# Whole products with diagonal blocks used in place, an earlier load, and two max terms on GpSimd, in a linear-attention and SwiGLU kernel

## The chip, the cores and the metric

The kernel runs on one core of a Trainium2 chip. The metric is the device time of one execution in microseconds (us), the slowest core's; here there is only one. A time is about 2 us longer than the span of the profile of the same execution. Engines are named as the profile names them: PE (TensorE matmuls), PEld (its weight loads), DVE (VectorE), ACT (ScalarE), POOL (GpSimd), SP.

## The reference

Linear attention over 8 batches, 8 heads, 576 positions and head size 64 feeds a SwiGLU block with 4608 tokens, width 512 and inner width 1536.

```python
phi = lambda x: np.where(x > 0, x, np.exp(x) - 1.0) + 1.0      # = max(x, 0) + min(exp(x), 1)
kv  = einsum('bhsd,bhse->bhde', phi(k), v);   z = phi(k).sum(axis=2)
att = einsum('bhsd,bhde->bhse', phi(q), kv) / (einsum('bhsd,bhd->bhs', phi(q), z) + 1e-6)
x   = att as [4608, 512]
out = (silu(x @ w_gate) * (x @ w_val)) @ w_out
```

## The kernel before

Tokens go through the SwiGLU block in 9 groups of 512. "Layer 1" is 12 blocks of 8 matmuls with 512 columns, "layer 2" is 4 x 12 such matmuls. Attention of the next batch is prepared between them. Batches 0 and 1 take their own path, because the kernel has to start before everything is loaded. GpSimd issues all loads, and each converts f32 to f16 on its way. The order of those issues in the source is the order of the queue.

phi of batch 0 is made from a max term (`kp[1]`) and a min term (`kp[0]`). For the first pair of heads (lp 0) they are added. For the second pair the product takes both terms, so it needs no sum:

```python
def term(src, dst, lp, val, op):
    nc.vector.tensor_scalar(out=dst[...strided...], in0=src[:, 2*lp:2*lp+2, :]..., scalar1=val, scalar2=None, op0=op)
def k_max(lp): term(k16[0], kp[1], lp, 0.0, ALU.max)
...
k_max(0); k_min(0); k_sum(0); q_max(0, 0); q_min(0); q_max(0, 1)   # DVE, batch 0
z0(0, 0); z0_copy(0, 0); warm(4, pX[1])                            # warm(): matmuls that only keep PE busy
t0(...); den0(0); q_min(1); t0(...); k_max(1); k_min(1)
... z0(0, 1); mm1(0, 0); r0_copies(0); den0(1); num0(0); mm1(0, 1); r0_copies(1)
```

`mm1` gives a 128 x 128 product for a pair of heads, of which only the two diagonal 64 x 64 blocks count. They are copied one by one into R:

```python
R = two([P, 4, D], FP16, "R")
def r_copies(b):
    for hh in range(2):
        for h2 in range(2):
            nc.scalar.activation(out=R[b % 2][rows, hh:4:2, :], in_=kvv[rows, :, c:c + D], func=AF.Copy, ...)
```

The loads, in order: k, q, v of batch 0 in halves; six pairs of `w_gate`/`w_val` column blocks with k and q of batch 1 between them; the first third of `wo`, v of batch 1, the other two thirds of `wo`, and then k of batch 2.

In group 0, layer 2 is cut into 12 pieces of 4 matmuls (three passes over four banks), and between them stand batch 1's product, its denominators (`den1`, each followed by ln and exp on ACT), numerators (`num1`) and the exp of batch 2's k:

```python
w = at(12, [... (2, mm1(1, 0)), (2, mm1(1, 1)), (2, r1_copies()), (3, t1(pX[0], 7, 9, A)), (3, exp_k(2, 0)),
    (4, den1(0)), (4, phi_k(2, 0)), (5, num1(0)), (5, exp_k(2, 1)), (6, den1(1)), (6, phi_k(2, 1)), (7, num1(1)), ...])
```

Of the kernel before, what the change touches and what calls it, by code (L numbers as in the profile page):

```python
# [13 lines left out]
P = 128  # L14
# [3 lines left out]
def kernel(  # L18
# [50 lines left out]
    R = two([P, 4, D], FP16, "R")  # L69
# [84 lines left out]
    def terms_k(b, lp):  # L154

        return (kp[1], kp[0]) if (b, lp) == (0, 1) else (kp[b % 2],)

    def mm1(b, lp):
        if lp == 0:
            kvb[b] = (bank(), bank()) if b > 1 else ((pV[2], pX[0]), (pX[2], pV[2]))[b]  # L160
        W = 2 * D + (b > 1)
        for j in range(J):
            for term in terms_k(b, lp):
                for hh in range(2):
                    rows = slice(C * hh, C * hh + C)
                    if b < 2:
                        vv = v16[b][rows, 2 * lp:2 * lp + 2, D * j:D * j + D]
                    else:
                        vv = vm[b % 2][rows, j, :, :].rearrange("p l c -> p (l c)")[:, 130 * lp:130 * lp + W]
                    nc.tensor.matmul(  # L170
                        out=kvb[b][hh][:, 256 * lp:256 * lp + W], lhsT=term[rows, j, P * lp:P * lp + P], rhs=vv,
                        start=(j == 0 and term is terms_k(b, lp)[0]), stop=(j == J - 1 and term is terms_k(b, lp)[-1]))
# [7 lines left out]
    def r_copies(b):  # L180
        for hh in range(2):
            kvv = kvb[b][hh][:, :].rearrange("p (i c) -> p i c", i=2)
            for h2 in range(2):
                rows, c = slice(D * h2, D * h2 + D), (D + (b > 1)) * h2
                nc.scalar.activation(
                    out=R[b % 2][rows, hh:4:2, :],
                    in_=kvv[rows, :, c:c + D], func=AF.Copy, bias=0.0, scale=1.0)
# [52 lines left out]
    def corners(ps, lhs, b, j0, j1, lps=(0, 1)):  # L240

        for lp in lps:
            for hh in range(2):
                for e in range(2):
                    rows = slice(D * e, D * e + D)
                    nc.tensor.matmul(out=ps[2 * lp + e][C * hh:C * hh + C, :], lhsT=lhs[rows, 2 * lp + hh, :],  # L246
                                     rhs=qT[b % 2][rows, j0:j1, lp, C * hh:C * hh + C], start=True, stop=True)

    def mm2(g, spare, engs):
        ps = [bank(), bank(), bank(), spare]  # L250
        us = units(g)
        c00 = 2 * C if g == 2 else 0
        for b in sorted(set(u[0] for u in us)):
            js = [j for (bb, j) in us if bb == b]
            c0 = C * us.index((b, js[0]))
            if b > 1:
                corners([x[:, c0:c0 + C * len(js)] for x in ps], R[b % 2], b, js[0], js[-1] + 1)
        for i in range(4):
            dst = xT[i][g % 2][:, c00:]
            if engs[i] == "A":  # L260
                nc.scalar.activation(out=dst, in_=ps[i][:, c00:], func=AF.Copy, bias=0.0, scale=1.0 / SC)
            else:
                nc.vector.tensor_scalar(out=dst, in0=ps[i][:, c00:], scalar1=1.0 / SC, scalar2=None, op0=ALU.mult)
# [79 lines left out]
    ld_w1(256, 512)  # L343
    ld_w1(512, 768)
    ld_k(1)
    ld_w1(768, 1024)
    ld_w1(1024, 1280)
    ld_q(1)
    ld_w1(1280, 1536)
    ld_w2(0)  # L350
    ld_v(1)
# [20 lines left out]
    def term(src, dst, lp, val, op):  # L372
        nc.vector.tensor_scalar(
            out=dst[:, :, P * lp:P * lp + P].rearrange("p j (s d) -> p s j d", d=D),
            in0=src[:, 2 * lp:2 * lp + 2, :].rearrange("p s (j d) -> p s j d", d=D), scalar1=val, scalar2=None, op0=op)

    def k_max(lp):
        term(k16[0], kp[1], lp, 0.0, ALU.max)
# [4 lines left out]
    def k_sum(lp):  # L383
        c = slice(P * lp, P * lp + P)
        nc.vector.tensor_tensor(out=kp[0][:, :, c], in0=kp[0][:, :, c], in1=kp[1][:, :, c], op=ALU.add)

    def q_max(b, lp):
        term(q16[b], qp[1], lp, 0.0, ALU.max)
# [6 lines left out]
    def z0(b, lp):  # L395
        ts = terms_k(b, lp)
# [27 lines left out]
    def r0_copies(lp):  # L424
        for hh in range(2):
            for e in range(2):
                rows, c = slice(D * e, D * e + D), 256 * lp + D * e
                nc.vector.tensor_copy(out=R[0][rows, 2 * lp + hh, :], in_=kvb[0][hh][rows, c:c + D])

# [12 lines left out]
    def den0(lp):  # L442
        corners({2 * lp + e: dbank0[e][:, :] for e in range(2)}, zz, 0, 0, 8, (lp,))
        ln0([b[:, :] for b in dbank0], rr[:, 2 * lp:2 * lp + 2, :])
        exp_neg(rr[:, 2 * lp:2 * lp + 2, :])

    def num0(lp):
        corners({2 * lp + e: nbank0[lp][e][:, :] for e in range(2)}, R[0], 0, 0, 8, (lp,))
# [6 lines left out]
    exp0(q16[0], eq, 1)  # L455
    k_max(0)
# [4 lines left out]
    q_max(0, 1)  # L461
# [13 lines left out]
    k_max(1)  # L475
    k_min(1)
    t0_copy(pV[0], 1, 0, 4, V)
    t0_copy(pV[1], 1, 4, 8, V)
    warm(3, pG[0])
    z0(0, 1)  # L480
    z0_copy(0, 1)
    mm1(0, 0)
    r0_copies(0)
    den0(1)
    warm(2, pG[0])
    num0(0)
    mm1(0, 1)
    r0_copies(1)
# [31 lines left out]
    def den1(lp):  # L520
        corners({2 * lp + e: dbank[e][:, 0:W7] for e in range(2)}, zz, 1, 0, 7, (lp,))
# [3 lines left out]
    def num1(lp):  # L525
        corners({2 * lp + e: nbank[e][:, 0:W7] for e in range(2)}, R[1], 1, 0, 7, (lp,))
# [5 lines left out]
    def den2():  # L532
        corners([dbank[m % 2][:, part1[m]] for m in range(4)], zz, 1, 7, 9)
# [3 lines left out]
    def num2():  # L537
        corners([nbank[m % 2][:, part1[m]] for m in range(4)], R[1], 1, 7, 9)
# [3 lines left out]
    def r1_copies():  # L542
        for hh in range(2):
            kvv = kvb[1][hh][:, :].rearrange("p (i c) -> p i c", i=2)
            for h2 in range(2):
                rows, c = slice(D * h2, D * h2 + D), D * h2
                nc.vector.tensor_copy(out=R[1][rows, hh:4:2, :], in_=kvv[rows, :, c:c + D])
# [8 lines left out]
    def first():  # L556
# [5 lines left out]
            (1, lambda: z0(1, 1)), (1, lambda: z0_copy(1, 0)), (1, lambda: z0_copy(1, 1)), (2, lambda: mm1(1, 0)),  # L562
            (2, lambda: mm1(1, 1)), (2, lambda: r1_copies()), (3, lambda: t1(pX[0], 7, 9, A)), (3, lambda: exp_k(2, 0)),
            (4, lambda: den1(0)), (4, lambda: phi_k(2, 0)), (5, lambda: num1(0)), (5, lambda: exp_k(2, 1)),
            (6, lambda: den1(1)), (6, lambda: phi_k(2, 1)), (7, lambda: num1(1)), (8, lambda: den2()),
            (9, lambda: num2()), (9, lambda: exp_q(2, 0)), (10, lambda: exp_q(2, 1))])
        return sl, w

    def steady(b, late=0):
# [4 lines left out]
            (3 + late, lambda: zb(b)), (3 + late, lambda: zb_copy(b)), (3 + late, lambda: s3_prod(b, 0)),  # L574
# [20 lines left out]
    for i in range(4):  # L595
# [3 lines left out]
        if i == 0:  # L599
            num0(1)  # L600
# [5 lines left out]
        if i == 2:  # L606
            d8 = [(pV[2], pX[0])[m % 2][:, part8[m]] for m in range(4)]
            n8 = [(pX[1], pX[2])[m % 2][:, part8[m]] for m in range(4)]
            corners(d8, zz, 0, 8, 9)
# [3 lines left out]
    corners(n8, R[0], 0, 8, 9)  # L613
    for m in range(4):
        x0(n8[m], r8[:, m % 2, part8[m]], xT[m][1][:, 0:C])
    ld_w2(1)
    ld_w2(2)
    ld_k(2)
# [21 lines left out]
    for g in range(1, NG):  # L640
# [3 lines left out]
        if b1 < B:  # L644
            sl, w = steady(b1, 1 if g == 1 else 0)
# [52 lines left out]
```

## Time and profile before

| | |
|---|---|
| time, median of the first 3 runs | 331.39 us (330.43 to 331.45) |
| PE busy | 97% of a span of 327.6 us |
| first layer-1 matmul | 17.89 us |
| layer 2 of group 0 starts | 40.38 us |
| layer 1 of group 1 starts | 59.06 us |
| layer 1 of group 2 starts | 93.21 us, and then each group takes 33.36 us |

The starts of stages are read from the PE timeline: the first matmul of each. From group 2 on there is nothing to win except by taking work from PE. What follows concerns the first 93 us. The execution that was profiled took 329.72 us at a mean clock of 1.00.

The page of the kernel before. First come span and busy PE, then the granted clock of PE in 40 slices (9 is 90% or more of full speed), and the chain that ended last, as shares of the span:

```profile
span 327.6 us, 5144 instructions
...
PE 317.6 (97%) x1980; PEld 150.6 (46%) x1980; DVE 216.4 (66%) x406; ACT 170.5 (52%) x251; POOL 31.6 (10%) x47
...
PEclk9999999999999999999999999999999999999999
...
PE 80%; DMA 8%; ACT 6%; DVE 3%; issue 2%; POOL 0%; SPq 0%; ACTq 0%; POOLq 0%
...
```

The timeline of DVE before, at the terms for lp 1 (start, duration, engine, source line, operation, out<-in, shapes):

```profile
12.11 0.74 DVE L373 TENSOR_SCALAR qp_73<-eq 128x1152 f16<-128x1152 f16 x1
12.76 0.44 DVE L373 TENSOR_SCALAR kp_72<-k_0_63 128x1152 f16<-128x1152 f16 x1
13.12 0.45 DVE L373 TENSOR_SCALAR kp_71<-ek 128x1152 f16<-128x1152 f16 x1
```

One max or min of 1152 elements costs DVE 0.45 us (the second line is the k max that the change moves); one of the three takes longer, here the first with 0.74.

The timeline of POOL before, where it issues the weight loads (in brackets: idle time before, and what ended it):

```profile
6.73 0.75 POOL L112 DMA_DIRECT2D wv<-in_moe_w_val_dram  x1
7.46 0.76 POOL L112 DMA_DIRECT2D wg<-in_moe_w_gate_dram  x1
8.99 0.75 POOL L112 DMA_DIRECT2D wv<-in_moe_w_val_dram  x1 [0.77 <-DMA q_0_65<-in_q_dram]
10.43 0.74 POOL L112 DMA_DIRECT2D wg<-in_moe_w_gate_dram  x1 [0.68 <-DMA q_0_65<-in_q_dram]
```

Eight loads are in flight here, and each further issue waits until one lands. The landings follow one another without a hole from 8.7 to 61 us, 1.33 us apart for a weight block, 2.64 for a third of `wo`.

The timeline of ACT before, in group 0's layer 2:

```profile
49.56 1.16 ACT L121 ACTIVATE ek<-k_0_63 128x1152 f16<-128x1152 f16 x1 [1.98 <-DMA k_0_63<-in_k_dram]
50.63 0.62 ACT L432 ACTIVATE rr<-pX_117,epst 128x448 f32<-128x448 f32 x1
```

The exp of batch 2's k waited 1.98 us for its load, which landed at 49.54, and the ln of batch 1's first denominators had to wait behind it.

The waits of PE before (out and line of the waiter, what it waited for, us in total, times, longest):

```profile
PE pX_117 L246 <- ACT rr L432: 0.9, 1, 0.9
PE pG_112 L274 <- ACT sil_100 L279: 0.9, 1, 0.9
```

The first is this ln. The second stands before 71.93 us in group 1: a SiLU queued on ACT behind the copies of R.

### The profile page before, as it was taken

The page shows a single profiled execution, that of the slowest core. Times are in us where ns is not written, and L with a number is a line of the kernel's source. Part 1 is how long each engine was busy: PE and PEld are TensorE (multiplying, and loading weights), DVE is VectorE, ACT ScalarE, POOL GpSimd, SP SyncE. Part 2 cuts the span into 40 slices and gives each one's busy share as a digit, 9 for nine tenths or more (in the row PEclk, how much of TensorE's full clock was granted, in tenths as well). Part 3 has the DMA queues.
Part 4 walks back from the last instruction along what each step waited for, and adds up shares of the span by engine and source line. Part 5 has one row for each costly group of instructions (what it writes and reads, how often), then busy time and mean ns, then how long its engine had stood idle before and what let it go on. Part 6 is the DMA issues. An engine that isn't in the chain of part 4 may idle for free.

```text
span 327.6 us, 5144 instructions
## 1 busy us (share of the span) xinstructions
PE 317.6 (97%) x1980; PEld 150.6 (46%) x1980; DVE 216.4 (66%) x406; ACT 170.5 (52%) x251; POOL 31.6 (10%) x47
## 2 busy tenths in 40 slices
PE   8899997989999999999999999999999999999994
PEld 6644452534444444444444444444444444444443
DVE  3757747679967986798579857985797344234321
ACT  2859949845745684568455844584431233123310
POOL 8454300010001000100010000000000000000000
PEclk9999999999999999999999999999999999999999
DMA  7999999986486448553846350134012410140014
GB/s 99 197 199 200 204 207 208 242 149 116 95 151 94 79 82 168 75 95 81 168 65 107 58 120 1 26 64 97 18 24 53 95 30 3 32 92 6 0 32 96
DMA packets 40984, 32.18 MB, mean 98 GB/s; under 512 B 16256, under 2 KB 36480, under 8 KB 40960
## 3 DMA queue, kind: packets, MB, share of 16 engines
q0 software_dynamic: 20640, 18.88, 37.0%
q1 hardware_dynamic: 20160, 12.85, 17.4%
q8 instruction: 15, 0.25, 0.3%
q10 hardware_dynamic: 160, 0.13, 0.2%
q14 instruction: 9, 0.07, 0.1%
HBM read 37.75 MB, written 9.44 MB: 144 GB/s over the span
## 4 chain that ended last, share of the span: by engine, by line
PE 80%; DMA 8%; ACT 6%; DVE 3%; issue 2%; POOL 0%; SPq 0%; ACTq 0%; POOLq 0%
PE pG_112 L274 12%; PE pG_113 L274 12%; PE pV_114 L274 8%; PE pV_115 L274 8%; PE pV_116 L274 8%; PE pV_115 L295 6%; PE pG_112 L295 6%; PE pV_114 L295 6%; PE pG_113 L295 6%; DMA k_0_63<-in_k_dram 6%; DMA q_0_65<-in_q_dram 2%; PE pX_118 L170 2%; PE pX_118 L246 1%; DMA out_dram<-osb_104 1%; ACT ek L121 1%
## 5 line engine op out<-in xcount | busy, mean ns | idle before, releaser
L274 PEld LDWEIGHTS <-wv 128*128 128x128 f16 x432 | 42.3, 98 | 51.0
L274 PEld LDWEIGHTS <-wg 128*128 128x128 f16 x432 | 41.3, 98 | 51.3 <-issue 2.7
L279 ACT ACTIVATE sil_100<-pG_112 128x512 f16<-128x512 f32 x51 | 30.5, 597 | 48.9 <-PE pG_112 L274 48.4
L279 ACT ACTIVATE sil_101<-pG_113 128x512 f16<-128x512 f32 x51 | 30.4, 596 | 36.9 <-PE pG_113 L274 35.2
L295 PEld LDWEIGHTS <-hT_98 128*128 128x128 f16 x228 | 21.3, 98 | 25.7 <-issue 1.5
L295 PEld LDWEIGHTS <-hT_99 128*128 128x128 f16 x192 | 18.5, 98 | 22.7 <-issue 0.9
L305 DVE TENSOR_SCALAR osb_104<-pV_115 128x512 f32<-128x512 f32 x9 | 6.2, 691 | 17.2 <-PE pV_115 L295 17.2
L214 DVE TENSOR_REDUCE den<-prod 128x12 f32<-128x768 f16 x18 | 17.0, 943 | 0.0
L295 PE MATMUL pV_114<-wo,hT_98 128*128 128x512 f16 x60 | 14.1, 379 | 0.2 <-DVE hT_98 L280 0.2
L295 PE MATMUL pV_115<-wo,hT_98 128*128 128x512 f16 x60 | 14.1, 380 | 0.0
L295 PE MATMUL pG_112<-wo,hT_98 128*128 128x512 f16 x60 | 14.1, 379 | 0.0
L303 ACT ACTIVATE osb_103<-pG_112 128x512 f32<-128x512 f32 x8 | 4.7, 584 | 16.3 <-PE pG_112 L295 16.3
L280 DVE SCALAR_TENSOR_TENSOR hT_98<-pV_114,sil_100 128x512 f16<-128x512 f32 x11 | 7.6, 688 | 7.7 <-PE pV_114 L274 5.5
L305 DVE TENSOR_SCALAR osb_105<-pG_113 128x512 f32<-128x512 f32 x8 | 5.5, 691 | 9.7 <-PE pG_113 L295 9.7
L295 PE MATMUL pG_113<-wo,hT_98 128*128 128x512 f16 x48 | 11.4, 380 | 0.0
L295 PE MATMUL pG_113<-wo,hT_99 128*128 128x512 f16 x48 | 11.1, 380 | 0.0
L295 PE MATMUL pV_114<-wo,hT_99 128*128 128x512 f16 x48 | 11.0, 379 | 0.0
L295 PE MATMUL pG_112<-wo,hT_99 128*128 128x512 f16 x48 | 11.0, 379 | 0.0
L295 PE MATMUL pV_115<-wo,hT_99 128*128 128x512 f16 x48 | 11.0, 379 | 0.0
L280 DVE SCALAR_TENSOR_TENSOR hT_98<-pV_114,sil_101 128x512 f16<-128x512 f32 x8 | 5.5, 692 | 8.1 <-ACT sil_101 L279 5.2
L274 PE MATMUL pG_112<-xT_0_90,wg 128*128 128x512 f16 x27 | 10.3, 380 | 0.0
L305 DVE TENSOR_SCALAR osb_102<-pV_114 128x512 f32<-128x512 f32 x9 | 6.2, 690 | 6.1 <-PE pV_114 L295 6.1
(240 smaller groups left out, 747.8 us busy)
## 6 DMA issues: line engine op xcount, KB each, us to landing
k_1_64<-in_k_dram POOLq DMA_DIRECT2D x4, 576.0 KB, 9.9
q_1_66<-in_q_dram POOLq DMA_DIRECT2D x4, 576.0 KB, 9.7
v_1_68<-in_v_dram POOLq DMA_DIRECT2D x4, 576.0 KB, 11.3
out_dram<-osb_102 SPq DMA_DIRECT2D x18, 128.0 KB, 2.4
out_dram<-osb_103 SPq DMA_DIRECT2D x18, 128.0 KB, 2.4
out_dram<-osb_104 SPq DMA_DIRECT2D x18, 128.0 KB, 2.4
out_dram<-osb_105 SPq DMA_DIRECT2D x16, 128.0 KB, 2.9
k_0_63<-in_k_dram POOLq DMA_DIRECT2D x3, 576.0 KB, 13.5
```

The source lines that it names most:

```text
L121: nc.scalar.activation(out=e[:, s, :], in_=src[b % 2][:, s, :], func=AF.Exp, bias=0.0, scale=1.0)
L170: nc.tensor.matmul(out=kvb[b][hh][:, 256 * lp:256 * lp + W], lhsT=term[rows, j, P * lp:P * lp + P], rhs=vv, start=(j == 0 and term is term ...
L214: nc.vector.tensor_reduce(out=den[:, HL * j0:HL * j1], in_=prod[:, 0:j1 - j0, :].rearrange("p j (l d) -> p (j l) d", d=D), axis=AX.X, op=A ...
L246: nc.tensor.matmul(out=ps[2 * lp + e][C * hh:C * hh + C, :], lhsT=lhs[rows, 2 * lp + hh, :], rhs=qT[b % 2][rows, j0:j1, lp, C * hh:C * hh ...
L274: nc.tensor.matmul(out=ps[:, :], lhsT=src[:, i, P * fb:P * fb + P], rhs=xT[i][g % 2][:, :], start=(i == 0), stop=(i == 3))
L279: nc.scalar.activation(out=s[:, :], in_=pg[:, :], func=AF.Silu, bias=0.0, scale=1.0)
L280: nc.vector.scalar_tensor_tensor(out=hT[g % 2][:, fb, :], in0=pv[:, :], scalar=SC, in1=s[:, :], op0=ALU.mult, op1=ALU.mult)
L295: nc.tensor.matmul(out=pso[(g, t)][:, :], lhsT=hT[g % 2][:, fb, P * t:P * t + P], rhs=wo[:, fb, :], start=(fb == 0), stop=(fb == FB - 1))
L303: nc.scalar.activation(out=o[:, :], in_=ps[:, :], func=AF.Copy, bias=0.0, scale=1.0 / SC)
L305: nc.vector.tensor_scalar(out=o[:, :], in0=ps[:, :], scalar1=1.0 / SC, scalar2=None, op0=ALU.mult)
```

## The change

It has four parts. (1) The products stay whole in R, and the diagonal blocks are used in place, so that half as many copies do. (2) The max terms of q and k for lp 1 in batch 0 go to GpSimd, and so does a new sum for lp 1, so that `mm1(0, 1)` takes one term. The start's order on PE changes with it, and two short `warm` calls go (5 matmuls). (3) k of batch 2 is loaded ahead of the last two thirds of `wo`, and work between group 0's layer-2 pieces is put in another order. (4) Batch 2's product, diagonals and copies come one slot later in group 1.

```diff
-    R = two([P, 4, D], FP16, "R")
+    R = two([P, 4, P + 1], FP16, "R")
...
-            for h2 in range(2):
-                nc.scalar.activation(out=R[b % 2][rows, hh:4:2, :], in_=kvv[rows, :, c:c + D], ...)
+            nc.scalar.activation(out=R[b % 2][:, hh:4:2, 0:W], in_=...[:, :, 0:W], ...)
+    def kv(b):
+        c1 = D + (b > 1)
+        return lambda i, e: R[b % 2][D * e:D * e + D, i, c1 * e:c1 * e + D]
...
+        term(k16[0], kp[1], lp, 0.0, ALU.max, (nc.vector, nc.gpsimd)[lp])          # k_max; q_max alike
+        (nc.vector, nc.gpsimd)[lp].tensor_tensor(out=kp[0]..., in0=kp[0]..., in1=kp[1]..., op=ALU.add)   # k_sum
...
     exp0(q16[0], eq, 1)
+    q_max(0, 1)
+    k_max(1)
+    ld_w1(256, 512)
...
+    mm1(0, 0)
+    z0(0, 1)
     t0_copy(...)
+    r0_copies(0)
+    z0_copy(0, 1)
+    k_sum(1)
+    ld_w1(512, 768)
+    ld_k(1)
...      (all other loads as before, and then)
+    ld_v(1)
+    ld_k(2)
+    ld_w2(1)
+    ld_w2(2)
+    num0(0)
...
-  (3, t1(pX[0], 7, 9, A)), (3, exp_k(2, 0)), (4, den1(0)), ..., (5, num1(0)), (5, exp_k(2, 1)), (6, den1(1)), ...
+  (2, t1(pX[0], 7, 9, A)), (2, mm1(1, 0)), (2, mm1(1, 1)), (2, r1_copies()), (2, exp_k(2, 0)), (2, exp_k(2, 1)),
+  (3, den1(0)), (3, phi_k(2, 0)), (4, num1(0)), (5, den1(1)), ...
...
-            sl, w = steady(b1, 1 if g == 1 else 0)
+            sl, w = steady(b1, 2 if g == 1 else 0)
```

More of the change, by code (lines that the diff above doesn't have):

```diff
@@ L152 @@
     kvb = {}
-    def terms_k(b, lp):
-        return (kp[1], kp[0]) if (b, lp) == (0, 1) else (kp[b % 2],)
     def mm1(b, lp):
@@ L162, in mm1 @@
         for j in range(J):
-            for term in terms_k(b, lp):
-                for hh in range(2):
-                    rows = slice(C * hh, C * hh + C)
-                    if b < 2:
-                        vv = v16[b][rows, 2 * lp:2 * lp + 2, D * j:D * j + D]
-                    else:
-                        vv = vm[b % 2][rows, j, :, :].rearrange("p l c -> p (l c)")[:, 130 * lp:130 * lp + W]
-                    nc.tensor.matmul(
-                        out=kvb[b][hh][:, 256 * lp:256 * lp + W], lhsT=term[rows, j, P * lp:P * lp + P], rhs=vv,
-                        start=(j == 0 and term is terms_k(b, lp)[0]), stop=(j == J - 1 and term is terms_k(b, lp)[-1]))
+            for hh in range(2):
+                rows = slice(C * hh, C * hh + C)
+                if b < 2:
+                    vv = v16[b][rows, 2 * lp:2 * lp + 2, D * j:D * j + D]
+                else:
+                    vv = vm[b % 2][rows, j, :, :].rearrange("p l c -> p (l c)")[:, 130 * lp:130 * lp + W]
+                nc.tensor.matmul(
+                    out=kvb[b][hh][:, 256 * lp:256 * lp + W], lhsT=kp[b % 2][rows, j, P * lp:P * lp + P], rhs=vv,
+                    start=(j == 0), stop=(j == J - 1))
     def zdiag(b, lp):
@@ L180, in r_copies, with zs @@
     def r_copies(b):
+        W = 2 * D + (b > 1)
         for hh in range(2):
-            kvv = kvb[b][hh][:, :].rearrange("p (i c) -> p i c", i=2)
-            for h2 in range(2):
-                rows, c = slice(D * h2, D * h2 + D), (D + (b > 1)) * h2
-                nc.scalar.activation(
-                    out=R[b % 2][rows, hh:4:2, :],
-                    in_=kvv[rows, :, c:c + D], func=AF.Copy, bias=0.0, scale=1.0)
+            nc.scalar.activation(out=R[b % 2][:, hh:4:2, 0:W],
+                                 in_=kvb[b][hh][:, :].rearrange("p (i c) -> p i c", i=2)[:, :, 0:W], func=AF.Copy,
+                                 bias=0.0, scale=1.0)
+    def kv(b):
+        c1 = D + (b > 1)
+        return lambda i, e: R[b % 2][D * e:D * e + D, i, c1 * e:c1 * e + D]
+    def zs(i, e):
+        return zz[D * e:D * e + D, i, :]
     zps = {}
@@ L245, in corners @@
                     rows = slice(D * e, D * e + D)
-                    nc.tensor.matmul(out=ps[2 * lp + e][C * hh:C * hh + C, :], lhsT=lhs[rows, 2 * lp + hh, :],
+                    nc.tensor.matmul(out=ps[2 * lp + e][C * hh:C * hh + C, :], lhsT=lhs(2 * lp + hh, e),
                                      rhs=qT[b % 2][rows, j0:j1, lp, C * hh:C * hh + C], start=True, stop=True)
@@ L256, in mm2 @@
             if b > 1:
-                corners([x[:, c0:c0 + C * len(js)] for x in ps], R[b % 2], b, js[0], js[-1] + 1)
+                corners([x[:, c0:c0 + C * len(js)] for x in ps], kv(b), b, js[0], js[-1] + 1)
         for i in range(4):
@@ L342 @@
     ld_w1(0, 256)
-    ld_w1(256, 512)
-    ld_w1(512, 768)
-    ld_k(1)
-    ld_w1(768, 1024)
-    ld_w1(1024, 1280)
-    ld_q(1)
-    ld_w1(1280, 1536)
-    ld_w2(0)
-    ld_v(1)
     nc.scalar.preload_act_table_set("natural_log_exp_and_others")
@@ L370, in exp0, with term @@
         nc.scalar.activation(out=e[:, 2 * lp:2 * lp + 2, :], in_=src[:, 2 * lp:2 * lp + 2, :], func=AF.Exp, bias=0.0, scale=1.0)
-    def term(src, dst, lp, val, op):
-        nc.vector.tensor_scalar(
+    def term(src, dst, lp, val, op, eng=nc.vector):
+        eng.tensor_scalar(
             out=dst[:, :, P * lp:P * lp + P].rearrange("p j (s d) -> p s j d", d=D),
@@ L377, in k_max @@
     def k_max(lp):
-        term(k16[0], kp[1], lp, 0.0, ALU.max)
+        term(k16[0], kp[1], lp, 0.0, ALU.max, (nc.vector, nc.gpsimd)[lp])
     def k_min(lp):
@@ L384, in k_sum @@
         c = slice(P * lp, P * lp + P)
-        nc.vector.tensor_tensor(out=kp[0][:, :, c], in0=kp[0][:, :, c], in1=kp[1][:, :, c], op=ALU.add)
+        (nc.vector, nc.gpsimd)[lp].tensor_tensor(out=kp[0][:, :, c], in0=kp[0][:, :, c], in1=kp[1][:, :, c], op=ALU.add)
     def q_max(b, lp):
-        term(q16[b], qp[1], lp, 0.0, ALU.max)
+        term(q16[b], qp[1], lp, 0.0, ALU.max, (nc.vector, nc.gpsimd)[lp])
     def q_min(lp):
@@ L395, in z0 @@
     def z0(b, lp):
-        ts = terms_k(b, lp)
+        ts = (kp[1], kp[0]) if (b, lp) == (0, 1) else (kp[b],)
         for j in range(J):
@@ L425, in r0_copies @@
         for hh in range(2):
-            for e in range(2):
-                rows, c = slice(D * e, D * e + D), 256 * lp + D * e
-                nc.vector.tensor_copy(out=R[0][rows, 2 * lp + hh, :], in_=kvb[0][hh][rows, c:c + D])
+            nc.vector.tensor_copy(out=R[0][:, 2 * lp + hh, 0:P], in_=kvb[0][hh][:, 256 * lp:256 * lp + P])
     def ln0(src, dst):
@@ L442, in den0 @@
     def den0(lp):
-        corners({2 * lp + e: dbank0[e][:, :] for e in range(2)}, zz, 0, 0, 8, (lp,))
+        corners({2 * lp + e: dbank0[e][:, :] for e in range(2)}, zs, 0, 0, 8, (lp,))
         ln0([b[:, :] for b in dbank0], rr[:, 2 * lp:2 * lp + 2, :])
@@ L447, in num0 @@
     def num0(lp):
-        corners({2 * lp + e: nbank0[lp][e][:, :] for e in range(2)}, R[0], 0, 0, 8, (lp,))
+        corners({2 * lp + e: nbank0[lp][e][:, :] for e in range(2)}, kv(0), 0, 0, 8, (lp,))
         for i in range(2 * lp, 2 * lp + 2):
@@ L460 @@
     q_min(0)
-    q_max(0, 1)
     z0(0, 0)
@@ L474 @@
     t0(pV[1], 1, 4, 8)
-    k_max(1)
     k_min(1)
+    mm1(0, 0)
+    z0(0, 1)
     t0_copy(pV[0], 1, 0, 4, V)
     t0_copy(pV[1], 1, 4, 8, V)
-    warm(3, pG[0])
-    z0(0, 1)
+    r0_copies(0)
     z0_copy(0, 1)
-    mm1(0, 0)
-    r0_copies(0)
+    k_sum(1)
+    ld_w1(512, 768)
+    ld_k(1)
+    ld_w1(768, 1024)
+    ld_w1(1024, 1280)
+    ld_q(1)
+    ld_w1(1280, 1536)
+    ld_w2(0)
+    ld_v(1)
[3 more added lines that the diff above has]
+    num0(0)
     den0(1)
-    warm(2, pG[0])
-    num0(0)
     mm1(0, 1)
-    r0_copies(1)
     def at(n, items):
@@ L520, in den1 @@
     def den1(lp):
-        corners({2 * lp + e: dbank[e][:, 0:W7] for e in range(2)}, zz, 1, 0, 7, (lp,))
+        corners({2 * lp + e: dbank[e][:, 0:W7] for e in range(2)}, zs, 1, 0, 7, (lp,))
         ln0([b[:, 0:W7] for b in dbank], rr[:, 2 * lp:2 * lp + 2, 0:W7])
@@ L525, in num1 @@
     def num1(lp):
-        corners({2 * lp + e: nbank[e][:, 0:W7] for e in range(2)}, R[1], 1, 0, 7, (lp,))
+        corners({2 * lp + e: nbank[e][:, 0:W7] for e in range(2)}, kv(1), 1, 0, 7, (lp,))
         for e in range(2):
@@ L532, in den2 @@
     def den2():
-        corners([dbank[m % 2][:, part1[m]] for m in range(4)], zz, 1, 7, 9)
+        corners([dbank[m % 2][:, part1[m]] for m in range(4)], zs, 1, 7, 9)
         ln0([b[:, 0:2 * W2] for b in dbank], r8[:, :, :])
@@ L537, in num2 @@
     def num2():
-        corners([nbank[m % 2][:, part1[m]] for m in range(4)], R[1], 1, 7, 9)
+        corners([nbank[m % 2][:, part1[m]] for m in range(4)], kv(1), 1, 7, 9)
         for m in range(4):
@@ L543, in r1_copies @@
         for hh in range(2):
-            kvv = kvb[1][hh][:, :].rearrange("p (i c) -> p i c", i=2)
-            for h2 in range(2):
-                rows, c = slice(D * h2, D * h2 + D), D * h2
-                nc.vector.tensor_copy(out=R[1][rows, hh:4:2, :], in_=kvv[rows, :, c:c + D])
+            nc.vector.tensor_copy(out=R[1][:, hh:4:2, 0:P],
+                                  in_=kvb[1][hh][:, :].rearrange("p (i c) -> p i c", i=2)[:, :, 0:P])
     def block(src, e, dst):
@@ L561, in first @@
             (0, lambda: t1(pX[0], 0, 4, A)), (1, lambda: t1(pX[1], 4, 7, V)), (1, lambda: z0(1, 0)),
-            (1, lambda: z0(1, 1)), (1, lambda: z0_copy(1, 0)), (1, lambda: z0_copy(1, 1)), (2, lambda: mm1(1, 0)),
-            (2, lambda: mm1(1, 1)), (2, lambda: r1_copies()), (3, lambda: t1(pX[0], 7, 9, A)), (3, lambda: exp_k(2, 0)),
-            (4, lambda: den1(0)), (4, lambda: phi_k(2, 0)), (5, lambda: num1(0)), (5, lambda: exp_k(2, 1)),
-            (6, lambda: den1(1)), (6, lambda: phi_k(2, 1)), (7, lambda: num1(1)), (8, lambda: den2()),
-            (9, lambda: num2()), (9, lambda: exp_q(2, 0)), (10, lambda: exp_q(2, 1))])
+            (1, lambda: z0(1, 1)), (1, lambda: z0_copy(1, 0)), (1, lambda: z0_copy(1, 1)),
+            (2, lambda: t1(pX[0], 7, 9, A)), (2, lambda: mm1(1, 0)), (2, lambda: mm1(1, 1)), (2, lambda: r1_copies()),
+            (2, lambda: exp_k(2, 0)), (2, lambda: exp_k(2, 1)), (3, lambda: den1(0)), (3, lambda: phi_k(2, 0)),
+            (4, lambda: num1(0)), (5, lambda: den1(1)), (5, lambda: phi_k(2, 1)), (6, lambda: num1(1)),
+            (7, lambda: den2()), (8, lambda: num2()), (9, lambda: exp_q(2, 0)), (10, lambda: exp_q(2, 1))])
         return sl, w
@@ L573, in steady @@
             (2, lambda: zdiag(b, 0)), (2, lambda: zdiag(b, 1)), (2, lambda: r_copies(b)),
-            (3 + late, lambda: zb(b)), (3 + late, lambda: zb_copy(b)), (3 + late, lambda: s3_prod(b, 0)),
+            (3 + (late > 0), lambda: zb(b)), (3 + (late > 0), lambda: zb_copy(b)), (3 + (late > 0), lambda: s3_prod(b, 0)),
             (4, lambda: s3_reduce(b, 0)), (5, lambda: s3_recip(b, 0)), (5, lambda: s3_prod(b, 1)),
@@ L599 @@
         if i == 0:
+            r0_copies(1)
             num0(1)
@@ L608 @@
             n8 = [(pX[1], pX[2])[m % 2][:, part8[m]] for m in range(4)]
-            corners(d8, zz, 0, 8, 9)
+            corners(d8, zs, 0, 8, 9)
             ln0([pV[2][:, 0:P], pX[0][:, 0:P]], r8[:, :, 0:P])
@@ L612 @@
     nc.scalar.preload_act_table_set("silu_and_others")
-    corners(n8, R[0], 0, 8, 9)
+    corners(n8, kv(0), 0, 8, 9)
     for m in range(4):
         x0(n8[m], r8[:, m % 2, part8[m]], xT[m][1][:, 0:C])
-    ld_w2(1)
-    ld_w2(2)
-    ld_k(2)
     sl, w = first()
```

## The prediction

> **What bounds it now.** The page shows PE busy 97% of a 327.6 us span at full clock; the chain of waits gives PE 80%, DMA 8%, ACT 6%. The PE timeline shows 512-column matmuls starting every 0.216 us. From 93.4 us on every group takes 33.36 us with no PE wait over 0.2 us. The losses lie earlier: (a) the first layer-1 matmul starts only at 17.89; (b) between 46.8 and 59.06, the second layer of group 0 interleaved with batch 1's denominators, starts stand apart by about 3 us more than their own work (gaps before 51.29, 51.82, 53.46, 53.99, 56.5, 57.07); (c) 1.06 us before 71.93, waiting for the first SiLU behind the R copies, which wait on DVE. In (b), k of batch 2 lands at 49.54 (18.3 us after issue) and its exp stands at 49.56 in front of batch 1's ln on ACT. Loads from 3.4 to about 61 us land one after another (1.33 us per 256 KB, 2.64 per wo third, 2.85 per 576 KB); order counts.
>
> **Change, costed.**
> - k(2) ahead of two wo thirds: 2 x 2.64 = 5.2 us earlier, 44.3. Both its exps then run before the ln's (ACT chain from about 45.5: 2.2 us exps, 2.0 us ln+exp per half). wo third 2 moves from 44.09 to about 47.0, just where PE wants it (46.78 before, some 47.2 with den1 moved ahead). New limit: the DVE chain phi_k (1.9) and x0 (1.2), two short PE waits of 0.8 left. Layer 1 of group 1 starts about 2 us earlier.
> - One slot later for batch 2's mm1, zdiag and R copies: SiLU no longer behind the copies; saves about 0.9 of the 1.06 us.
> - R copies halved (ACT 4 x 0.28 to 2 x about 0.45; DVE likewise): only in (a)-(c); under 0.3 us.
> - GpSimd: q and k max (lp 1) leave DVE (2 x 0.46), mm1(0,1) halves to 18 weight pairs (-0.5 us). Estimate (the trace has no such op) from the Trainium skill, GPSIMD Engine Reference, section 3.1 (about 1 cycle per element for one input, 2.6 for two, 1.2 GHz): max 1.0-1.5 us, sum 2.5 us or more. The skill's SBUF page, "Who interferes with whom", calls the port shared with VectorE an exclusive lock, so DVE's fast q_min(1) at 12.1 may wait until k_max ends (13-14). The sum also must wait for z0(0,1), which reads its target: 15.3-18. mm1(0,1), ahead of layer 1 on PE, then starts near 18: layer 1 starts 18.2-19, not 17.9. And GpSimd issues the loads: those behind the sum go out at 17.7-18.5, where a gapless queue needs 17.1. I expect a hole of about 0.8 us in the loads.
>
> So (a) loses about 0.5, (b) wins 1.5-2, (c) 0.9, rest 0.2.
>
> **Prediction:** 328.8 us, 326.7 to 331.3 8 in 10. Faster by over 2%: 0.04; within 2%: 0.93; slower: 0.03.
>
> **What would show it.** k(2) lands at 44-46; the wait before 71.93 mostly gone; layer 1 of group 1 starts at 57-58; first layer-1 matmul at 18-19; GpSimd sum 2-3 us and DVE q_min held until k_max ends; period of later groups 33.36 still.
>
> **What would make it wrong.** GpSimd ops twice as long: loads and start slip 2 us or more, and the gain goes. GpSimd near DVE speed and no lock: start 1 us earlier, about 327. wo third 2 late: PE waits before the fifth layer-2 group. Loads of R at an odd column slowing PE in all groups.

## The result, and the profile after

331.51 us median (331.50 to 332.03, 4 runs) against 331.04 us (330.43 to 331.45, 4 runs) of the kernel before. The ratio is 1.002, with a 95% interval of 0.9998 to 1.0041: the two are the same, or the changed kernel is slower by a hair. Here and below a ratio is the mean time of one kernel's fast runs over the mean of the other's in the same rounds, so it is not quite the ratio of the medians.

The page of the changed kernel:

```profile
span 329.4 us, 5083 instructions
...
PE 317.2 (96%) x1957; PEld 150.0 (46%) x1957; DVE 220.0 (67%) x398; ACT 167.6 (51%) x239; POOL 40.5 (12%) x50
...
PEclk9969999999999999999999999999999999999999
...
PE 82%; ACT 5%; DVE 5%; issue 3%; DMA 2%; POOL 1%; SPq 0%; ACTq 0%; POOLq 0%; DVEq 0%
...
```

Two things stand out. DMA has nearly left the chain, from 8% to 2%: the chain no longer runs through the load of batch 2's k. That alone doesn't prove that the early load did its work, since a later start also leaves the load more time; experiments 2 and 11 take the two apart. And in the third slice the clock of PE fell. By the clock records it was at half from 18.66 to 25.48 us.

| first matmul of | before | after | difference | by which stage |
|---|---|---|---|---|
| layer 1, group 0 | 17.89 | 21.22 | +3.33 | start |
| its third block | 22.76 | 27.91 | +5.15 | +1.82, at half clock |
| layer 2, group 0 | 40.38 | 45.53 | +5.15 | 0 |
| layer 1, group 1 | 59.06 | 61.76 | +2.70 | -2.45, layer 2 of group 0 |
| layer 1, group 2 | 93.21 | 94.85 | +1.64 | -1.06, group 1 |
| layer 1, group 3 | 126.57 | 128.21 | +1.64 | 0: 33.36 us a group, as before |

In this comparison the last parts of the change won 3.5 us, and the start lost 5.15. The 1.64 us that remain are more than the timed difference of about 0.5, because the first profile of before was a fast one (experiment 6).

The timeline of POOL after:

```profile
6.74 0.75 POOL L112 DMA_DIRECT2D wv<-in_moe_w_val_dram  x1
9.77 3.12 POOL L365 TENSOR_SCALAR qp_74<-q_0_65 128x1152 f16<-128x1152 f16 x1 [2.28 <-DMA q_0_65<-in_q_dram]
12.89 3.29 POOL L365 TENSOR_SCALAR kp_72<-k_0_63 128x1152 f16<-128x1152 f16 x1
16.13 0.81 POOL L112 DMA_DIRECT2D wg<-in_moe_w_gate_dram  x1
16.94 0.75 POOL L112 DMA_DIRECT2D wv<-in_moe_w_val_dram  x1
17.69 2.39 POOL L377 TENSOR_TENSOR kp_71<-kp_71,kp_72 128x1152 f16<-128x1152 f16 x1
20.01 0.78 POOL L112 DMA_DIRECT2D wg<-in_moe_w_gate_dram  x1
```

What took DVE 0.45 us takes GpSimd 3.12 and 3.29. Meanwhile GpSimd issues nothing: the load that went out at 7.46 before goes out at 16.13. The queue ran down to a single load, the one that landed at 17.29, and k of batch 1 landed at 29.73 instead of 25.30.

The timeline of DVE after:

```profile
10.99 2.21 DVE L365 TENSOR_SCALAR qp_73<-eq 128x1152 f16<-128x1152 f16 x1
13.13 3.36 DVE L365 TENSOR_SCALAR kp_71<-ek 128x1152 f16<-128x1152 f16 x1
```

These are the two min operations that stayed on DVE. Each ends some 0.3 us after the GpSimd operation beside it: 13.20 after 12.89, 16.49 after 16.18. DVE did not gain the 0.9 us of the two max terms; it lost 4.4 us by being held.

The waits of PE after:

```profile
PE pG_112 L393 <- POOL kp_72 L365: 1.3, 1, 1.3
PE pV_116 L165 <- POOL kp_71 L377: 1.3, 1, 1.3
PE pV_114 L405 <- POOL qp_74 L365: 1.0, 1, 1.0
```

PE waits for each of the three GpSimd operations in turn. The view of windows shows what this does to the clock, first before and then after (columns: stretch, length, busy time of PE, PEld, DVE, ACT, POOL with instruction counts, clock, DMA share, GB/s):

```profile
11.00:18.00 7.00, 6.68 (x138) 4.64 (x136) 5.86 (x16) 6.40 (x9) 3.71 (x6) 1.00 1.38 199
21.20:25.30 4.10, 4.10 (x34) 1.79 (x33) 1.19 (x5) 3.41 (x6) 1.48 (x2) 1.00 1.29 203
```

```profile
11.00:18.00 7.00, 3.20 (x76) 2.37 (x76) 7.00 (x8) 3.76 (x5) 6.99 (x5) 1.00 0.90 130
21.20:25.30 4.10, 4.10 (x15) 1.17 (x14) 1.78 (x4) 0.00 (x0) 4.10 (x7) 0.50 1.13 134
```

Between 11 and 18 us PE was busy for 3.20 us instead of 6.68. In the stretch from 21.2, where layer 1 has begun, it ran at clock 0.50, and 512-column matmuls started 0.43 us apart instead of 0.216. The loads moved 130 GB/s instead of 199. The Trainium skill tells of this gate in "TensorE: Matmul & The Clock Gate", Part 1: after an idle window of about 3.4 us PE runs at half clock, and the window runs freely. The trace agrees on the length: the stretch at half clock lasted 6.83 us, which is twice 3.41. But no such window was wholly idle here: in the 3.41 us before the clock fell at 18.65, PE was busy for 1.59 us.

The timeline of ACT after, where the exps of batch 2's k are:

```profile
50.55 2.21 ACT L121 ACTIVATE ek<-k_0_63 128x1152 f16<-128x1152 f16 x2
52.66 0.63 ACT L422 ACTIVATE rr<-pX_117,epst 128x448 f32<-128x448 f32 x1
```

No wait for a load stands before the exps now; k of batch 2 had landed at 49.03. Its issue no longer stands behind two thirds of `wo`, but all loads are later by 4.4 us, so it landed hardly earlier than the 49.54 of before.

### The profile page after: what moved, and what is told of

The parts are those of the page before. It is cut to its first block, busy times and chain, and to the rows that moved or that the text cites. A ratio compares the mean times of both kernels' runs of the same rounds, so it can differ in the third digit from the quotient of the medians.

```text
span 329.4 us, 5083 instructions
## 1 busy us (share of the span) xinstructions
PE 317.2 (96%) x1957; PEld 150.0 (46%) x1957; DVE 220.0 (67%) x398; ACT 167.6 (51%) x239; POOL 40.5 (12%) x50
## 4 chain that ended last, share of the span: by engine, by line
PE 82%; ACT 5%; DVE 5%; issue 3%; DMA 2%; POOL 1%; SPq 0%; ACTq 0%; POOLq 0%; DVEq 0%
PE pG_112 L275 13%; PE pG_113 L275 12%; PE pV_114 L275 8%; PE pV_115 L275 8%; PE pV_116 L275 8%; PE pV_115 L296 7%; PE pG_112 L296 7%; PE pV_114 L296 7%; PE pG_113 L296 6%; DMA q_0_65<-in_q_dram 2%; PE pX_118 L165 2%; DVE hT_98 L281 1%; DVE kp_71 L365 1%; ACT ek L121 1%; ACT sil_100 L280 1%
## 5 line engine op out<-in xcount | busy, mean ns | idle before, releaser
L306 DVE TENSOR_SCALAR osb_104<-pV_115 128x512 f32<-128x512 f32 x9 | 6.2, 689 | 16.8 <-PE pV_115 L296 16.8
L281 DVE SCALAR_TENSOR_TENSOR hT_98<-pV_114,sil_100 128x512 f16<-128x512 f32 x11 | 7.6, 691 | 8.4 <-PE pV_114 L275 6.3
L306 DVE TENSOR_SCALAR osb_105<-pG_113 128x512 f32<-128x512 f32 x8 | 5.5, 691 | 9.4 <-PE pG_113 L296 9.4
L275 PE MATMUL pG_113<-xT_0_90,wg 128*128 128x512 f16 x27 | 10.5, 388 | 0.0
L275 PE MATMUL pG_113<-xT_0_92,wg 128*128 128x512 f16 x27 | 10.5, 388 | 0.0
L275 PE MATMUL pG_112<-xT_0_90,wg 128*128 128x512 f16 x27 | 10.5, 388 | 0.0
```

Source lines behind the costliest of these rows:

```text
L275: nc.tensor.matmul(out=ps[:, :], lhsT=src[:, i, P * fb:P * fb + P], rhs=xT[i][g % 2][:, :], start=(i == 0), stop=(i == 3))
L281: nc.vector.scalar_tensor_tensor(out=hT[g % 2][:, fb, :], in0=pv[:, :], scalar=SC, in1=s[:, :], op0=ALU.mult, op1=ALU.mult)
L306: nc.vector.tensor_scalar(out=o[:, :], in0=ps[:, :], scalar1=1.0 / SC, scalar2=None, op0=ALU.mult)
```

## The experiments

The theory after the result was G: the GpSimd operations cost the start, by their length, by the port that they share with DVE, by the loads that they hold up, and by the clock. The rivals: L, the new order of PE work and loads in the start costs it, whichever engine does the terms; and W, the later win exists only because a late start gave the loads time.

### 1 and 7. The terms back on VectorE, all else as changed

```diff
-        term(k16[0], kp[1], lp, 0.0, ALU.max, (nc.vector, nc.gpsimd)[lp])
+        term(k16[0], kp[1], lp, 0.0, ALU.max)                    # q_max and k_sum alike
-    q_max(0, 1)
-    k_max(1)
     ld_w1(256, 512)
...
     q_min(0)
+    q_max(0, 1)
...
+    k_max(1)
     k_min(1)
```

> The changed kernel with its three GpSimd operations (q max, k max and the k sum of heads pair 1) back on VectorE, at the places in VectorE's order that they had before; all else as changed. Theory G (the three GpSimd operations, 3.1 to 3.3 us each for the max, cost the start: they block VectorE, hold back the loads, leave PE idle and so halve its clock): first layer-1 matmul at 17.0 to 17.9 us instead of 21.2, no stretch at half clock, second layer of group 0 at 40.0 to 40.6 instead of 45.5, k of batch 2 landing near 44.4 and the second wo third near 47.0; time 327.0 to 328.5, so about 3.5 under the changed kernel. Rival L (the new order of PE work and of loads in the start costs it, whichever engine does the terms): first layer-1 matmul stays after 20, time 330 to 331.5.

326.12 us median, ratio to before 0.9859 (0.9836 to 0.9882). One of its four executions, the profiled one, fell into an abnormal slow state (844.46 us; matmuls of 512 columns started about 0.6 us apart, and its trace holds no clock records). Why is not known. It is left out, and the kernel was run again for its trace:

> The first experiment again, since its profiled run had fallen into an abnormally slow state (842 us) and gave no usable trace. Expected as its timed runs: 325.3 to 326.5; layer 1 starts at 16.5 to 17.5, PE waits about 1.1 us for the second wo third, no half clock.

325.91 us (325.59 to 326.11), ratio 0.9852 (0.9823 to 0.9880). The first layer-1 matmul started at 15.90, no stretch was at half clock, and layer 2 of group 0 started at 39.62. Both expectations had layer 1 later than that, and the first one's time was 1 us or more too long. The windows of this run:

```profile
11.00:18.00 7.00, 5.13 (x107) 3.25 (x104) 5.83 (x15) 5.75 (x8) 3.08 (x5) 1.00 1.38 197
21.20:25.30 4.10, 4.10 (x28) 1.79 (x26) 1.91 (x6) 3.71 (x7) 1.48 (x2) 1.00 1.30 203
```

So it is the engine and not the order: rival L falls. The `warm` calls that the change dropped are missing here too, so they are not the cause either. Against before, the changed kernel stands at 1.002 and this one at 0.9852, so the three GpSimd operations cost 1.002 - 0.9852 = 1.7%, 5.6 us (5.3 with the 0.9859 of the first try; the ratios are from different rounds). One more thing is to be read here: the start at 15.90 was too early for the weights. The waits of PE show 1.2 us for a `wv` block that landed at 17.68, so layer 1's third block came at 22.00 all the same.

### 2. The start of the changed kernel alone

The diff is the start of the change; R, the load of batch 2's k, the order in layer 2 and the slots are as before.

> The start of the changed kernel alone (terms on GpSimd, single-term product, its order of PE work), with everything later as before: corner copies, k of batch 2 after the wo thirds, the old order of group 0's second layer, the old slots. Theory G: start as in the changed kernel (layer 1 at 21.2, half clock from about 18.7 to 25.5, second layer at 45.5), loads about 4.6 us late, so k of batch 2 lands near 54 and nothing is won later; time 335 to 337. Rival (the start's loss is partly absorbed by the waits of the later stage): 332 to 334.

334.57 us, ratio 1.0127 (1.0105 to 1.0149): 4.2 us over before, between the 335 to 337 of the theory and the 332 to 334 of the rival. The start is that of the changed kernel (21.0, half clock for 6.83 us from 18.38, layer 2 at 45.27), k of batch 2 landed at 53.93, and group 1 started at 63.45. So part of the 5 us was taken up by waits that the kernel before had anyway, as the rival said.

### 3. The order alone

```diff
+    ld_k(2)
     ld_w2(1)
     ld_w2(2)
-    ld_k(2)
...  (the new list of work in group 0's layer 2, and the later slots in group 1)
```

> The kernel before with only the orders changed: k of batch 2 ahead of two wo thirds, the new order of work between group 0's second-layer pieces, and batch 2's product and copies one slot later. Theory: start as before (17.9 and 40.4), group 1 starts at 56.0 to 57.2 instead of 59.06, the 1.06 us wait near 72 goes; time 3.0 to 3.8 us under before, 327.3 to 328.3. Rival W (the win in the changed kernel came only because its late start gave the loads time; with an early start the wo thirds arrive late and PE waits for them): group 1 starts at 58 to 59, time 329.5 to 331.

325.63 us, ratio 0.9849 (0.9832 to 0.9866): 5.0 us, more than the theory had. k of batch 2 landed at 44.64 and group 1 started at 56.25. Rival W was partly right. The waits of PE in this run have this line:

```profile
PE pV L295 <- DMA wo<-in_moe_w_out_dram: 1.1, 1, 1.1
```

The second `wo` third, at 47.33, is the new limit, and PE waits 1.1 us for it. It does not take the win away. Experiment 7, which has the whole change except GpSimd, wins no more than this (0.9852): the rest of the change gains nothing that can be told.

### 4. The changed kernel, with PE kept busy

```diff
+    warm(8, pG[0])
     q_min(1)
...
     mm1(0, 0)
+    warm(12, pG[0])
     z0(0, 1)
...
+    warm(5, pG[0])
     num0(0)
     den0(1)
+    warm(12, pG[0])
     mm1(0, 1)
```

> The changed kernel with 37 idle-filling matmuls of 256 columns in the four places where PE waited between 10 and 20 us; nothing else. Theory (PE's idle time brought the half clock of 18.7 to 25.5 us): no half clock, layer 1 still starts near 21.2, its third block starts near 26.1 instead of 27.9, time about 1.8 us less, 329.4 to 330.2. Rival (the half clock has another cause, or the filling delays the work as much as it saves): half clock still there, or time within 0.5 of the changed kernel.

330.21 us, ratio 0.9996 (0.9973 to 1.0018), so 0.8 us less than the changed kernel by the ratios, which is less than the expected 1.8 and not clear of the two intervals. (The two profiled executions differ by 1.3 us, 330.22 against 331.51.) The windows of this run:

```profile
11.00:18.00 7.00, 5.56 (x97) 4.18 (x96) 6.98 (x9) 3.39 (x5) 7.00 (x5) 1.00 0.95 134
21.20:25.30 4.10, 4.10 (x31) 1.72 (x32) 2.17 (x6) 0.87 (x3) 4.10 (x6) 1.00 1.19 144
```

The half clock is gone although POOL and DVE do just what they did, and layer 1 still starts at 21.13. So PE's own idle time brought it. The third block came at 25.84 instead of 27.91 and layer 2 at 43.45 instead of 45.53, which is the 1.8 us and a bit more. But then PE waited 1.3 us for the second third of `wo`, landing at 51.57, because the loads were as late as ever. That is why less than the 2.1 us of layer 2's start arrived at the end. What is shown here is the cause of the half clock; the gain in time is not.

### 5. The operations by themselves

In the kernel before, GpSimd also does these on scratch tiles after its last load (the order in the trace is the one here), and DVE goes on with its work:

```python
term(k16[0], kp[1], 1, 0.0, ALU.max, nc.gpsimd)                                    # strided output, 1152
nc.gpsimd.tensor_scalar(out=ek[:, 0:2, :], in0=q16[0][:, 0:2, :], scalar1=0.0, ..., op0=ALU.max)   # contiguous
nc.gpsimd.tensor_scalar(out=ek[:, 2:3, :], in0=q16[0][:, 2:3, :], ..., op0=ALU.max)                # 576
nc.gpsimd.tensor_tensor(...128x1152..., op=ALU.add)
nc.gpsimd.tensor_scalar(out=ek[:, 0:2, :], in0=q16[0][:, 0:2, :], scalar1=1.0, ..., op0=ALU.mult)
nc.gpsimd.tensor_copy(out=q16[1][:, 0:2, :], in_=v16[1][:, 0:2, :])
```

> The kernel before, with GpSimd operations on scratch tiles in the last group, when no load is issued: the same max of 1152 f16 elements with the strided output, the same with both sides contiguous, half of it contiguous, a two-input add of 1152, a multiply by a constant of 1152 contiguous, a copy of 1152; and VectorE's own 0.46 us max on other tiles beside them. Theory (a one-input tensor_scalar costs GpSimd some 2.7 ns per element whatever the pattern): strided and contiguous max and the multiply 3.0 to 3.3 us each, half 1.5 to 1.7, add 2.3 to 2.5. Rival P (the strided pattern, the loads' issue or VectorE beside it made it slow): contiguous max at 1.0 to 1.6 us. VectorE's max on unrelated tiles that comes up while a GpSimd operation runs ends only with it (1.5 to 3 us instead of 0.46), while VectorE operations with PSUM input stay at 0.69; if the wait at the start was one for data, it stays at 0.46.

The timeline of POOL in this run:

```profile
232.49 3.13 POOL L373 TENSOR_SCALAR kp<-k 128x1152 f16<-128x1152 f16 x1 [62.53 <-PE pX L170]
235.63 3.28 POOL L653 TENSOR_SCALAR ek<-q 128x1152 f16<-128x1152 f16 x1
238.89 1.90 POOL L654 TENSOR_SCALAR ek<-q 128x576 f16<-128x576 f16 x1
260.81 2.36 POOL L655 TENSOR_TENSOR kp<-kp,qp 128x1152 f16<-128x1152 f16 x1 [20.02 <-DVE qp L227]
263.15 3.13 POOL L656 TENSOR_SCALAR ek<-q 128x1152 f16<-128x1152 f16 x1
266.24 1.13 POOL L657 COPY q<-v 128x1152 f16<-128x1152 f16 x1
```

The max takes 3.13 us strided and 3.28 contiguous with no load being issued, and a multiply takes the same, during which DVE was idle (from 261.91 to 266.40). It is the operation, not the pattern or the surroundings: rival P falls. Nor do 3.13 and 3.28 differ by the pattern: in the changed kernel the first and the second max, both strided, took 3.12 and 3.29. From 576 to 1152 elements it grows by 3.28 - 1.90 = 1.38 us, 2.4 ns an element, a rough figure, since DVE operations ran beside both. An add with two inputs is quicker (2.36), and a copy far quicker (1.13).

They ran earlier than meant, beside group 6's work. That was luck, for it put DVE operations on quite other tiles (`eq`, `qp`, q of batch 7) next to them. The timeline of DVE there, and then the same two in the kernel before:

```profile
232.68 3.27 DVE L125 TENSOR_SCALAR eq<-eq 128x1152 f16<-128x1152 f16 x1
235.98 4.45 DVE L127 SCALAR_TENSOR_TENSOR qp<-q,eq 128x576 f16<-128x576 f16 x2
```

```profile
231.63 0.45 DVE L125 TENSOR_SCALAR eq<-eq 128x1152 f16<-128x1152 f16 x1
232.12 1.43 DVE L127 SCALAR_TENSOR_TENSOR qp_74<-q_1_66,eq 128x576 f16<-128x576 f16 x2
```

0.45 became 3.27 and 1.43 became 4.45, with no tile in common. So data was not what held DVE in the start. A shared access to SBUF, held by one engine for a whole instruction, fits the first two of these three operations, which end 0.3 to 0.4 us after the GpSimd operation beside them (235.95 after 235.62, 239.29 after 238.91). It doesn't fit the third, the second of the pair:

```profile
239.21 1.21 DVE L127 SCALAR_TENSOR_TENSOR qp<-q,eq 128x576 f16<-128x576 f16 x1
```

It took 1.21 us instead of some 0.7 and ended at 240.42, before the shorter max beside it (238.89 to 240.79). Why stays open; the profiler's spans on GpSimd are called rough. DVE's own max, which I had put in to see this, ran where GpSimd was idle and stayed at 0.45, so that part of the experiment told nothing. Operations with PSUM input (the 0.69 us ones) were not stretched, as one at 261.22 beside the add. The whole kernel took 338.86 us in its one run (state unknown), PE waited 5.8 us for the DVE work behind these, and its clock then was at half for 6.83 us.

### 6. The kernel before, profiled again

> The kernel before, unchanged, for a second profile: the order change alone won 5.0 us of time, but its profile shows only 1.8 (group 0's second layer) + 1.07 (one slot later) from the places it touches, and 1.0 from an earlier first layer 1, whose code is the same. If the first profile of before was a lucky one, this one has second-layer start to group 1 over 18.7 us (19.5 or more); if the rest is chance in the first load, that span is 18.7 again and only the start moves.

330.71 us (2 runs), ratio 0.9998. This time the first layer-1 matmul started at 16.96 and layer 2 at 39.45, both 0.93 earlier than in the first profile. That follows the loads: both halves of q had landed 0.7 us earlier, and in all six profiles with this start (before and experiments 3, 6, 10, 11, 12) the first layer-1 matmul comes 8.9 to 9.2 us after the first half of q. Group 1 still started at 59.94. From layer 2's start to group 1 it took 20.49 us instead of 18.68. The view of windows, first in the first profile and then in this one:

```profile
54.00:57.40 3.40, 3.08 (x28) 1.27 (x28) 3.27 (x6) 3.34 (x7) 0.74 (x1) 1.00 1.21 206
```

```profile
54.00:57.40 3.40, 3.37 (x17) 1.03 (x17) 3.27 (x6) 2.40 (x5) 0.74 (x1) 0.51 1.22 208
```

k of batch 2 landed at 49.58, as in the first profile. An earlier start only made PE wait longer for it (1.9 instead of 0.9 us in one go), and this time a stretch at half clock followed the wait. The wait alone doesn't decide it: in the profile of experiment 10, with the same code up to here, PE waited 1.7 us and the clock stayed full. Of the 25 further runs of the kernel before in these rounds, 23 had a mean clock of 0.986 to 0.996 and only two one of 1.00, so the first profile was the rare one. The whole 5.0 us of experiment 3 are found against this profile: 20.49 to 16.86 in layer 2 (3.6) and 34.39 to 33.08 in group 1 (1.3). The changed kernel, too, adds up against this profile: its start is 6.1 us later (45.53 against 39.45), layer 2 of group 0 takes 4.3 less (16.23 against 20.49) and group 1 1.3 less, which leaves 0.5, the timed difference.

### 8. A try for a better kernel

Experiment 3, with k of batch 2 loaded in halves and the second third of `wo` between them:

```diff
-    ld_k(2)
+    ld_k_half(2, 0)
     ld_w2(1)
+    ld_k_half(2, 1)
     ld_w2(2)
...
-    (2, exp_k(2, 0)), (2, exp_k(2, 1)), (3, den1(0)), (3, phi_k(2, 0)), (4, num1(0)), (5, den1(1)), ...
+    (2, exp_k(2, 0)), (3, den1(0)), (3, phi_k(2, 0)), (4, num1(0)), (4, exp_k(2, 1)), (5, den1(1)), ...
```

> A try for a better kernel: the order change alone, with k of batch 2 loaded in two halves, the second wo third between them, and the exp of the second half moved behind the first half's ln and exp. Theory (in the order change PE waits 1.1 us for the second wo third, which lands at 47.3): wo third lands near 45.9, that wait goes, group 1 starts at 54.7 to 55.8 instead of 56.25, time 324.2 to 325.2. Rival: the second exp on ACT delays the denominators as much, time 325.3 to 326.

325.00 us (324.81 to 325.25), ratio 0.9825 (0.9802 to 0.9849). The wait for `wo` is gone, the third landed at 45.38, and group 1 started at 55.65. This is the fastest of all kernels here. Experiment 3 had 0.9849 in other rounds, so the step from it is about 0.2% and not clear of the two intervals.

### 9. Whole products alone

The diff is part (1) of the change.

> The kernel before with only the products kept whole (half as many copies, diagonal blocks used in place). Theory: the copies of group 1's R on ACT take 2 x 0.39 instead of 4 x 0.28 us, so the wait before the seventh block of group 1 (1.06 and 1.21 us in the two profiles of before) shrinks by about 0.4; the earlier stages are pinned by the landing of k of batch 2, so nothing else moves; period of later groups 33.36 us; time 0 to 0.6 us under before. Rival: weights read at an odd column slow PE in every later group: period over 33.4, time over before.

330.33 us, ratio 0.9990 (0.9968 to 1.0013): no difference that can be told. The two copies of R on ACT take 0.66 us together where the four took 1.11 (from 70.14 to 71.26), the wait before the seventh block is 0.5 instead of 0.9 to 1.1 in the view of waits (1.06 to 1.21 by the starts of the matmuls), and a later group takes 33.36 us. The odd column did not slow PE.

### 10. Slots alone

> The kernel before with only batch 2's product, diagonals and copies one slot later in group 1. Theory: the wait before the seventh block (1.06 to 1.21 us) goes, nothing else changes; group 1 to group 2 takes 33.1 us instead of 34.15 to 34.39; time 1.0 to 1.3 us under before.

328.98 us, ratio 0.9953 (0.9929 to 0.9977): 1.6 us. Group 1 to group 2 took 33.08 us instead of 34.15 to 34.39, as expected, and the rest is within the interval.

### 11 and 12. The early load without the new order, and the new order without the early load

> The kernel before with only k of batch 2 loaded ahead of the last two wo thirds. Theory: it lands near 44.6 instead of 49.5, its exp no longer holds up the ln of batch 1's denominators, PE waits about 1.3 us for the second wo third instead, the half-clock stretch of the second profile of before does not come; group 1 starts at 56.5 to 58 instead of 59.1 to 59.9; time 2 to 3.5 us under before. Rival (the load order pays only together with the new order of work): less than 1 us.

327.94 us, ratio 0.9917 (0.9892 to 0.9942): 2.7 us. k of batch 2 landed at 44.23, group 1 started at 56.84, PE waited 0.7 us for the second third of `wo`, and its clock stayed full.

> The kernel before with only the new order of work between group 0's second-layer pieces, k of batch 2 still loaded last. Theory (the load's landing is the limit): both exps now stand in front of all the ln's on ACT and wait for the landing at 49.5, the first ln starts near 51.8 instead of 50.6, PE waits longer and at half clock; group 1 starts at 60.5 to 62; time 1 to 3 us over before. Rival (the order of work is what pays): under before.

331.76 us, ratio 1.0037 (1.0009 to 1.0066). The timeline of ACT says why:

```profile
49.56 2.21 ACT L121 ACTIVATE ek<-k 128x1152 f16<-128x1152 f16 x2 [4.40 <-DMA k<-in_k_dram]
```

Both exps now stand in front of every ln and wait 4.40 us for the load. Group 1 started at 60.83. The loss, 1.2 us, is at the low end of what was expected. So the landing of k is what the stage hung on. Without the load the order loses. Whether it adds anything to the load is not shown: 2.7 us for the load and 1.6 for the slots make 4.3, together with the order it is 5.0, and the difference of 0.7 is within the intervals.

## Why the prediction was wrong

It foretold 328.8 us (326.7 to 331.3) and it was 331.51. Going through it:

- **Where the gain lies (b), (c): right.** It had 1.5 to 2 us for layer 2 of group 0 and 0.9 for group 1; between the two first profiles it was 2.45 and 1.06. Taken alone, these parts win even more (5.0 us, experiment 3), because the profile read for the prediction was a rare run of the kernel before: its start was 0.9 us late, and the wait in layer 2 did not halve the clock. The prediction took that one profile as typical.
- **The step that failed: "max 1.0-1.5 us", and with it "(a) loses about 0.5".** The max measured 3.12 and 3.29 us, and 3.13 to 3.28 on scratch tiles (experiment 5); the start lost 5.15, of which 3.33 came before layer 1 and 1.82 from the half clock. The prediction worked the max out from the Trainium skill, "GPSIMD Engine Reference", section 3.1, taking for one input its figure of about one cycle per element, which stands there without the name of an operation. That fits the copy (1.13 us) and not a `tensor_scalar`. The sum, predicted at "2.5 us or more", took 2.39.
- **"layer 1 starts 18.2-19": 21.2.** The chain that the prediction wrote down was right in its order, max, held DVE, sum behind `z0(0,1)`, product, layer 1; it was fed with max operations too short by 3.4 to 4.4 us in sum (3.12 + 3.29 against 2 to 3). One link was another than it had: `z0(0,1)` was done by 17.21, and the sum began at 17.69 only because two load issues stand before it on GpSimd.
- **The lock: right.** The skill's "SBUF — State Buffer", section "Who interferes with whom", says that DVE in a two-port mode or with two SBUF inputs and GpSimd exclude each other for a whole instruction. 0.45 became 3.36 us in the start and 3.27 us in experiment 5, on unrelated tiles; one operation of experiment 5 is an exception.
- **"a hole of about 0.8 us in the loads": it was 4.4** (k of batch 1, 29.73 instead of 25.30), so k of batch 2 landed at 49.03 and not at 44 to 46. It did little harm by itself, since PE was as late as the loads; experiment 4 shows that it would be the next limit.
- **Not foreseen at all: the half clock.** PE was busy for 3.20 us of 7, and layer 1 then began at half speed: 1.82 us lost in the profile. "Loads and start slip 2 us or more, and the gain goes" was named among the ways to be wrong, but the clock was not.
- **R copies "under 0.3 us" and a period of 33.36 us: right** (experiment 9; 94.85 to 128.21).

Added up by the timed ratios: the GpSimd operations cost 5.6 us on top of everything else, and without them the same change would have won 4.8 us. The order's gain and the GpSimd loss are not simply additive: alone they are -5.0 and +4.2 us, together +0.5 or so (an interval that reaches zero). A late start takes away some of the waiting for batch 2's k that the order would have removed.

One thing stays open: how the 5.15 us of the start split between the held DVE, the length of the operations for PE, and the late loads. These can't be separated here, since one engine's operation makes all three. Only the clock's part, 1.8 us of it in the profile, was taken out by itself.

## What to carry to other kernels

An engine that is idle 90% of the time is not free: ask what else it does (here it issues every load), what it shares with the engine that is to be relieved, and how long the very operation takes on it, measured once by itself. When work is moved in a place where PE has no other work, count the PE idle time that it makes, because some of it may be paid a second time at half clock (here 3.8 us of idle time between 11 and 18 us, and then 1.8 us more). And profile the kernel before twice before reading microseconds from its start: a stage that hangs on a load's landing hides what happens ahead of it, both gains and losses (here an early start of 0.9 us was lost in the wait for k of batch 2).

## What the Trainium skill lacked or had wrong

- "GPSIMD Engine Reference", section 4.1, has one-input operations at roughly line rate. The copy was (1.13 us for 1152 f16 elements), but a `tensor_scalar` max or multiply of the same size took 3.13 to 3.28 us, longer than the two-input add (2.36 us), and no figure for it stands in section 3.1.
- "TensorE: Matmul & The Clock Gate", Part 1, has the window of 3.4 us, and the runs agree (stretches of 3.41 and 6.83 us). It does not say how much idle time in a window is enough in a kernel that is not quite idle: here 3.20 us busy out of 7 brought it on, and the same code came with it (2.27 us between two matmul starts in experiment 6) and without it (1.30 us in the first profile, 2.08 in experiment 10).
- "SBUF — State Buffer", "Who interferes with whom", agrees with what was seen but for one operation (experiment 5: the second `scalar_tensor_tensor` of a pair ended at 240.42, inside a GpSimd max from 238.89 to 240.79). For two SBUF inputs there is now a size: a pair of f16 `scalar_tensor_tensor` went from 1.43 to 4.45 us beside GpSimd.
